# Batch 2 of a fused attention and MLP kernel: q loaded in plain form, cast by GpSimd and turned by TensorE

## The chip, the cores and the metric

The kernel runs on one core of one Trainium2 chip. The metric is the device time of one execution in microseconds (us), lower is better. The core has five engines that work side by side, each with its own queue of instructions that it takes strictly in order: TensorE (PE: matmuls and transposes by matmul; its weight loads are shown apart as PEld), VectorE (DVE), ScalarE (ACT), GpSimd (POOL) and SyncE (SP). They wait for one another by semaphores. Transfers (DMAs) are issued from an engine's queue; here SP issues plain and transposing transfers, and POOL issues those that cast float32 to bfloat16 on the way.

## The reference

Decayed causal attention, and then a SiLU MLP on its output:

```python
# q, k, v: 8 batches x 8 heads x 576 tokens x 64; f: 8 x 8 x 576
scores = (1 / sqrt(64)) * q @ k.T
cum = cumsum(log(clip(f, 1e-4, 1)))            # along the tokens
scores = where(causal, -1e9, scores + cum[:, None] - cum[None, :])
attn = softmax(scores)
x = (attn @ v), heads side by side             # 4608 tokens x 512
h = x @ w_in                                   # 512 x 2048
out = (h * sigmoid(h)) @ w_out                 # 2048 x 512 -> 4608 x 512, float32
```

## The kernel before

**Tiling.** Two heads of one batch make a pair, whose 2 x 64 columns fill 128 partitions. There are 32 pairs, p = 0 to 31; batch b holds pairs 4b to 4b+3. The 576 tokens of a head are five blocks of 128, 128, 128, 128 and 64. The scores are made transposed (keys on partitions, queries along the free axis), so q and k are needed with the head dimension on partitions: tiles qT (two buffers, one per batch) and kT (two constant tiles, by turns). `scores(p, t)` (L267) makes one of four groups t of score blocks by matmul (L278), which ScalarE turns into exponentials (L303). `attend_rows` (L334) multiplies them with v, which GpSimd has scaled by the decay and given a column of ones (`prep_v`, L243). The result is divided by its row sum on VectorE (L355, L356) and turned into columns of xT, by TensorE (`turn_pair`, L363, with ScalarE copies L374) in the first batches. xT is cut into nine groups g of 512 tokens for the MLP: `m1_chunk` (L388) makes one of 16 chunks of a group's hidden layer (four matmuls L397, tanh on ScalarE L408, product on VectorE L409), `m2_part` (L416) a quarter of one output tile of 128 tokens (four matmuls L422, then ScalarE L431 and a store by SP, L435).

**How q and k come to be turned.** Batches 0 and 1 (`NEARLY = 2`) take the first way: `load_main` and `load_tail` load them from SP as float32, tokens on partitions, rows of 1 KB, into a tile `whole` (q and k side by side, from the two buffers tagged gtile that later hold the hidden layer too) and a tile `raw` for the last 64 tokens. `cast_both` (L556) has GpSimd cast a pair's q and k to bfloat16 (L190 the main part, L199 the tail). `transposes(p, which)` (L224) has TensorE turn five blocks (L232) into a PSUM tile tpqk of the four buffers tagged big, and VectorE copies that into qT or kT (L237, L241). Batches 2 to 7 take the second way: `load_qk` (L120) loads one block of all eight heads from POOL's queue with a cast to bfloat16 into a tile mp, and `turn_qk` (L128) has SP issue a transposing transfer from mp into qT or kT (L132).

**The order of the work** is written out by hand, in `manual_schedule`: the order in the program is the order on each engine. After pairs 0 to 3 a loop over p = 4 to 31 (L639) takes each pair through: transfers planned for this p (the table `plan`: turns, loads of v), `scores(p, 0)` and `(p, 1)`, some MLP work, for p up to 6 `transposes(p + 1, 0)`, `attend_rows(p - 1)`, `prep_v(p + 1)`, for p up to 5 `cast_both(p + 2)`, the POOL loads planned for this p (the table `fetch`), `scores(p, 2)` and `(p, 3)`, and more MLP work. `pace` says how many MLP pieces a pair gets. `can_m1` lets the first half of a group's MLP run at most two groups ahead of the second half. For batch 2, the fetches stand at p = 4 (blocks 0 and 1) and p = 5 (blocks 2, 3, 4), the turns at p = 6 and p = 7, and the first use at p = 8.

Of the kernel before, what the change touches and what calls it, by code (L numbers as in the profile page):

```python
# [19 lines left out]
def kernel(  # L20
# [12 lines left out]
    B, H, S, D = q.shape  # L33
# [9 lines left out]
    NPB = H // 2  # L43
# [28 lines left out]
    tpool = ctx.enter_context(tc.tile_pool(name="tpool", bufs=3))  # L72
    opool = ctx.enter_context(tc.tile_pool(name="opool", bufs=4))
    NEARLY = 2
    NTURN = 4
    LAG = 10.0
    MOST = 9.0
# [8 lines left out]
    def raw_tile():  # L86
        return stp.tile([P, DM], FP32, name="raw", tag="raw")
# [4 lines left out]
    def load_main(b, h0, h1):  # L92
        if b not in whole:
            whole[b] = gpool.tile(
                [P, 2, H, (NB - 1) * D], FP32, name="whole", tag="gtile"
            )
        for which, src in enumerate((q, k)):
            nc.sync.dma_start(  # L98
                out=whole[b][:, which, h0:h1, :],
                in_=src[b, h0:h1, 0:SM, :].rearrange("h (p c) d -> p h (c d)", c=NB - 1),  # L100
            )

    def load_tail(b):
        for which, src in enumerate((q, k)):
            t = raw_tile()
            tails[b, which] = t.rearrange("s (h d) -> s h d", h=H)
            nc.sync.dma_start(
                out=tails[b, which][:TAIL, :, :],
                in_=src[b, :, SM:S, :].rearrange("h s d -> s h d"),
            )  # L110
# [86 lines left out]
    def cast_tail(b, j, which):  # L197
        m = cast[b, j, which]
        nc.gpsimd.tensor_copy(  # L199
            out=m[:TAIL, NB - 1, :, :], in_=tails[b, which][:TAIL, 2 * j : 2 * j + 2, :]  # L200
        )
# [236 lines left out]
    m2_queue = [(g, tb, pt) for g in range(NG) for tb in range(4) for pt in range(4)]  # L438
    m1_ready = 0
# [16 lines left out]
    def can_m1():  # L456
        if not m1_queue:
            return False
        g = m1_queue[0][0]
        return g < m1_ready and (not m2_queue or m2_queue[0][0] > g - 2)  # L460

    def can_m2():
        return bool(m2_queue) and (not m1_queue or m1_queue[0][0] > m2_queue[0][0])
# [14 lines left out]
    def have():  # L478
        return sum(1 for x in m1_queue + m2_queue if x[0] < m1_ready)

    def pace(p):
        b, j = divmod(p, NPB)
        if b < NEARLY:
            return have() / (NPB - j)
# [32 lines left out]
    def add(to, at, fn, *args):  # L517
        to.setdefault(at, []).append(lambda: fn(*args))

    for b in range(NEARLY, B):  # L520
        for i, group in enumerate([(0, 1), (2,), (3, 4)]):
            at = NPB * b - 4 + min(i, 1) if b == NEARLY else NPB * b - 7 + i
            for c in group:
                for w in range(2):
                    add(fetch, at, load_qk, b, c, w)
                    if b <= NEARLY + 1:
                        add(plan, at + (2 if b == NEARLY else 3), turn_qk, b, c, w)
                    elif i == 0 and b - 2 >= NTURN:
                        add(plan, NPB * b - 4, defer, 9.0, partial(turn_qk, b, c, w))
                    else:  # L530
                        add(plan, NPB * b - 4 + min(i, 1), turn_qk, b, c, w)
                add(plan, NPB * b - 5 + i + (b == NEARLY), load_v, b, c, nc.sync)

# [11 lines left out]
    with tc.manual_schedule():  # L545
        nc.scalar.dma_start(out=f_sb[:, :], in_=f.rearrange("b h s -> (b h) s"))
        load_main(0, 0, 2)
        load_tail(0)
        load_main(0, 2, 4)
        for c in range(2):  # L550
            load_v(0, c, nc.sync)
        load_main(0, 4, H)
        for c in range(2, NB):
            load_v(0, c, nc.sync)

        def cast_both(p):  # L556
            b, j = divmod(p, NPB)
            for w in range(2):
                cast_main(b, j, w)
            for w in range(2):  # L560
                cast_tail(b, j, w)

        make_identity(nc, ident_bf)
        make_upper_triangular(nc, mask01, val=1.0, diag=True)
        make_identity(nc, ident_f)
        for kT in kTs:
            nc.vector.memset(kT[:, :, S:], 0.0)
        for u in us:
            nc.vector.memset(u[:, :, uoff[4] + TAIL :], 0.0)
        for va in vaugs:  # L570
            nc.vector.memset(va[:, NB - 1, :, :], 0.0)
        nc.vector.memset(wT[:, NB - 1, :], 0.0)
        nc.vector.tensor_scalar(
            out=maskadd[:, :], in0=mask01[:, :], scalar1=1.0, scalar2=1e30,
            op0=ALU.subtract, op1=ALU.mult,
        )
        decay_clip()
        LO, HI = ((0, 3),), ((3, NB),)
        for w in range(2):
            cast_main(0, 0, w)  # L580
        for w in range(2):
            cast_tail(0, 0, w)
        cast_both(1)
        cast_both(2)
        load_w(w_in_bf, moe_w_in, 0, DFF // 2)
        load_w(w_in_bf, moe_w_in, DFF // 2, DFF)
        for w in range(2):
            turn_first(w)
        scores(0, 0)
        turn_first_tails()  # L590
        scores(0, 1)
        decay_sum()
        scores(0, 3)
        transposes(1, 0)
        scores(0, 2)
        decay_turn()
        prep_v(0)
        transposes(1, 1)
        scores(1, 0)
        cast_both(3)  # L600
        load_tail(1)
        load_main(1, 0, 4)
        load_main(1, 4, H)
        for c in range(NB):
            load_v(1, c, nc.sync)
        for p in range(1, NPB):
            more = p + 1 < NPB
            prep_v(p)
            scores(p, 1)
            if more:  # L610
                transposes(p + 1, 0)
            scores(p, 3)
            if more:
                transposes(p + 1, 1)
            if p > 1:
                turn_pair(p - 2)
            attend_rows(p - 1, LO)
            scores(p, 2)
            if more:
                scores(p + 1, 0)  # L620
            attend_rows(p - 1, HI)
        turn_pair(NPB - 2)
        attend_rows(NPB - 1, LO)
        attend_rows(NPB - 1, HI)
        m1_chunk(0, 0, begin=True)
        turn_pair(NPB - 1)
        m1_ready = 1
        cast_both(NPB)
        cast_both(NPB + 1)
        prep_v(NPB)  # L630
        for c in range(0, NFC, NFC // 4):
            load_rows(w_out_bf, moe_w_out, c, c + NFC // 4)
        work(HOLD)
        transposes(NPB, 0)
        work(1)
        transposes(NPB, 1)
        work(2)
        due = 0.0
        for p in range(NPB, NP):  # L639
            b, j = divmod(p, NPB)  # L640
            early = b < NEARLY
            for fn in plan.get(p, []):
                fn()
            due += pace(p)
            n = int(due)
            due -= n
            n1, n2 = (n + 2) // 3, (n + 1) // 3
            n3 = n - n1 - n2
            scores(p, 0)
            scores(p, 1)  # L650
            spend(0.4)
            work(n1)
            ahead = p + 1 < NPB * NEARLY
            rows = NPB < p < NPB * NEARLY
            if ahead:
                transposes(p + 1, 0)
            if rows:
                attend_rows(p - 1, LO)
                spend(0.6)
            if p + 1 < NP:  # L660
                prep_v(p + 1)
            if p + 2 < NPB * NEARLY:
                cast_both(p + 2)
            for fn in fetch.get(p, []):
                fn()
            if early:
                work(n2 // 2)
            scores(p, 2)
            scores(p, 3)
            spend(0.3)  # L670
            if ahead:
                transposes(p + 1, 1)
            if rows:
                attend_rows(p - 1, HI)
            work(n2 - n2 // 2 if early else n2)
            if b >= NEARLY and j > 0:
                attend_rows(p - 1)
                spend(1.2)
            work(n3)
            if j > 0 and b < NTURN:  # L680
                turn_pair(p - 1)
            if j == NPB - 1:
                attend_rows(p)
                spend(1.2)
                if b < NTURN:
                    work(2)
                    turn_pair(p)
                    ready(p)
                else:
                    retire(p)  # L690
        while m1_queue or m2_queue or later:
            n = len(m1_queue) + len(m2_queue)
            work(1)
            if n == len(m1_queue) + len(m2_queue):
                spend(1.0)
# [28 lines left out]
```

## Time and profile before

| | |
|---|---|
| median of 3 runs | 363.94 us (363.58 to 365.53) |
| the profiled execution | 366.61 us, of which the profile's span is 364.8 us |
| mean granted TensorE clock in it | 0.984 |
| PE busy | 339.6 us (93% of the span) |
| ACT, DVE, POOL busy | 212.1, 189.7, 120.5 us |

The profiled execution is 2.7 us longer than the median of the runs, and 1.8 us of it lie outside the span. In the views below a line of the timeline holds the start, the duration, the engine, the line of the kernel, the operation and its tiles, the count, and in brackets how long the engine had been idle before and what ended that. A DMA issue on a queue (SPq, POOLq, POOL) shows the issuing, not the transfer. The line PEclk is the clock that was granted to TensorE in each of 40 equal slices of the span, in tenths of full speed.

### The profile page before, as it was taken

Reading aid. Unit: us, or ns where it says so; the run is one execution under the profiler, and the core shown is the slowest. Engines: PE = TensorE matmul, PEld = TensorE weight load, DVE = VectorE, ACT = ScalarE, POOL = GpSimd, SP = SyncE. Lnnn points to the kernel's source line nnn. Section 1 sums busy time; section 2 is a strip of 40 time slices with the busy share of each in tenths; the row PEclk is TensorE's granted clock in tenths of the full one; section 3 lists DMA queues with packets and bytes.
Section 4 is the critical chain, followed back from the end, with each engine's and each line's share of the span. In section 5 each row is a group of like instructions: output and inputs, shape, how many; then the busy total and the mean of one; then the engine's idle time right before and its main releaser. Section 6 shows DMA issues by size and latency. Waiting matters only on the chain.

```text
span 364.8 us, 7023 instructions
## 1 busy us (share of the span) xinstructions
PE 339.6 (93%) x2677; PEld 167.1 (46%) x2677; DVE 189.7 (52%) x442; ACT 212.1 (58%) x345; POOL 120.5 (33%) x204
## 2 busy tenths in 40 slices
PE   2798979947999999999999999999999999999995
PEld 1355435522455545554454444444544454444442
DVE  4764894422763387236832784358436832843410
ACT  4566764624974687567746784667367723744421
POOL 5563499466035704561454362011301000000000
PEclk9999999985999999999999999999999999999999
DMA  8899899999969799879979998453050014000012
GB/s 220 200 207 313 186 187 178 132 159 208 192 63 159 110 178 120 102 53 193 158 79 184 125 120 184 106 105 102 30 124 29 2 58 118 8 31 29 29 64 82
DMA packets 148082, 44.92 MB, mean 123 GB/s; under 512 B 136208, under 2 KB 142352, under 8 KB 148048
## 3 DMA queue, kind: packets, MB, share of 16 engines
q1 hardware_dynamic: 88544, 33.05, 42.3%
q0 software_dynamic: 59424, 11.28, 41.1%
q8 instruction: 21, 0.34, 0.4%
q10 hardware_dynamic: 80, 0.15, 0.1%
q14 instruction: 13, 0.11, 0.1%
HBM read 36.85 MB, written 9.44 MB: 127 GB/s over the span
## 4 chain that ended last, share of the span: by engine, by line
PE 75%; DMA 10%; SPq 7%; ACT 2%; POOL 2%; issue 1%; DVE 1%; ACTq 0%; DVEq 0%
PE hp L397 31%; PE po L422 31%; PE sc L278 6%; PE avr L346 6%; DMA w_out_bf<-in_moe_w_out_dram 3%; SPq L115 3%; DMA mp<-in_k_dram 3%; SPq L98 3%; SPq L132 2%; DMA qT<-mp 2%; ACT uT L303 1%; DMA vm<-in_v_dram 1%; DMA whole<-in_k_dram 1%; PE tpx L368 1%; POOL vaug L248 1%
## 5 line engine op out<-in xcount | busy, mean ns | idle before, releaser
L397 PE MATMUL hp<-xT,w_in_bf 128*128 128x512 bf16 x576 | 139.5, 385 | 1.1 <-ACT xT L374 0.7
L422 PE MATMUL po<-w_out_bf,gtile 128*128 128x512 bf16 x576 | 136.6, 379 | 0.9 <-DVE gtile L409 0.6
L409 DVE SCALAR_TENSOR_TENSOR gtile<-th,hp 128x512 bf16<-128x512 bf16 x144 | 96.3, 685 | 55.3 <-ACT th L408 53.1
L303 ACT ACTIVATE uT<-sc 128x1024 bf16<-128x1024 f32 (+1 forms) x128 | 101.2, 849 | 30.3 <-PE sc L278 21.6
L408 ACT ACTIVATE th<-hp 128x512 bf16<-128x512 f32 x144 | 85.0, 612 | 51.0 <-PE hp L397 48.2
L248 POOL TENSOR_TENSOR vaug<-vm,wT 128x512 bf16<-128x512 f32 x64 | 45.5, 733 | 140.7 <-PE avr L346 120.3
L397 PEld LDWEIGHTS <-w_in_bf 128*128 128x128 bf16 x576 | 53.5, 99 | 65.7 <-issue 8.6
L422 PEld LDWEIGHTS <-gtile 128*128 128x128 bf16 x576 | 53.6, 98 | 63.6 <-issue 3.2
L317 DVE TENSOR_TENSOR uT<-uT,mask 128x256 bf16<-128x256 bf16 (+1 forms) x112 | 35.8, 341 | 72.8 <-ACT uT L303 72.6
L431 ACT ACTIVATE osb<-po 128x512 f32<-128x512 f32 x36 | 21.7, 602 | 47.3 <-PE po L422 47.3
L278 PE MATMUL sc<-qT,kT 64*128 64x64 bf16 (+4 forms) x384 | 37.6, 288 | 12.2 <-DMA qT<-mp 6.5
L346 PEld LDWEIGHTS <-uT 128*128 128x128 bf16 x960 | 33.7, 98 | 7.1 <-issue 1.3
L346 PE MATMUL avr<-vaug,uT 128*128 128x65 bf16 x960 | 36.2, 195 | 0.7 <-POOL vaug L256 0.7
L278 PEld LDWEIGHTS <-kT 64*128 64x128 bf16 x384 | 15.1, 95 | 38.8 <-issue 24.0
L356 DVE TENSOR_TENSOR xt<-avr,rr 128x384 bf16<-128x384 f32 x64 | 31.4, 491 | 2.3
L123 POOL DMA_DIRECT2D mp<-in_q_dram x30 | 26.6, 887 | 0.0
L123 POOL DMA_DIRECT2D mp<-in_k_dram x30 | 25.9, 862 | 0.3 <-PE sc L278 0.3
L355 DVE RECIPROCAL rr<-avr 128x6 f32<-128x6 f32 x64 | 11.6, 182 | 19.0 <-PE avr L346 18.8
L374 ACT COPY xT<-tpx 128x512 bf16<-128x512 bf16 (+7 forms) x32 | 11.2, 404 | 17.2 <-PE tpx L368 17.2
L190 POOL CAST m<-whole 128x512 bf16<-128x512 f32 x16 | 9.8, 628 | 15.2 <-DMA whole<-in_q_dram 12.1
L368 PE MATMUL tpx<-ident_bf,xt 128*128 128x128 bf16 (+1 forms) x80 | 9.0, 216 | 1.3 <-DVE xt L356 1.1
L368 PEld LDWEIGHTS <-xt 128*128 128x128 bf16 (+1 forms) x80 | 6.2, 96 | 6.5 <-DVE xt L356 2.3
(47 smaller groups left out, 65.4 us busy)
## 6 DMA issues: line engine op xcount, KB each, us to landing
out_dram<-osb SPq DMA_DIRECT2D x36, 256.0 KB, 2.2
vm<-in_v_dram SPq DMA_DIRECT2D x32, 256.0 KB, 5.0
mp<-in_q_dram POOLq DMA_DIRECT2D x24, 128.0 KB, 5.5
mp<-in_k_dram POOLq DMA_DIRECT2D x24, 128.0 KB, 6.2
w_in_bf<-in_moe_w_in_dram POOLq DMA_DIRECT2D x2, 1024.0 KB, 11.2
w_out_bf<-in_moe_w_out_dram POOLq DMA_DIRECT2D x4, 512.0 KB, 9.7
whole<-in_q_dram SPq DMA_DIRECT2D x3, 512.0 KB, 10.9
whole<-in_k_dram SPq DMA_DIRECT2D x3, 512.0 KB, 9.6
```

The costliest lines, as they stand in the source:

```text
L123: nc.gpsimd.dma_start(out=t[: bs[c], :].rearrange("p (h d) -> p h d", h=H), in_=(q, k)[which][b, :, c * P : c * P + bs[c], :].rearrange("h ...
L248: nc.gpsimd.tensor_tensor(out=va[:n, c0:c1, :, 0:D], in0=vm[:n, c0:c1, 2 * j : 2 * j + 2, :], in1=wT[:n, c0:c1, 2 * j + b * H : 2 * j + 2 ...
L278: nc.tensor.matmul(sc[:, i, col : col + n], lhsT=kT[r, kb * P : (kb + 1) * P], rhs=qT[r, q0 : q0 + n], start=True, stop=not pe_adds,)
L303: nc.scalar.activation(out=u[:, :, o : o + col], in_=sc[:, :, 0:col], func=ACT.Exp, scale=scale)
L317: nc.vector.tensor_tensor(out=d, in0=d, in1=mk, op=ALU.mult)
L346: nc.tensor.matmul(av[:, qb - lo, i, :], lhsT=u[:, i, o : o + P], rhs=va[:, kb, i, :], start=(kb == 0), stop=(kb == qb),)
L356: nc.vector.tensor_tensor(out=xt[:, lo:hi, 2 * j : 2 * j + 2, :], in0=av[:, :, :, 0:D], in1=r[:, 0:n, :, None].to_broadcast([P, n, 2, D]), ...
L397: nc.tensor.matmul(hp[:, :], lhsT=w_in_bf[:, cc, fc * P : (fc + 1) * P], rhs=xg[g][:, cc, :], start=(cc == 0), stop=(cc == NCC - 1),)
L408: nc.scalar.activation(out=th[:, :], in_=hp[:, :], func=ACT.Tanh, scale=0.5)
L409: nc.vector.scalar_tensor_tensor(out=gte[:, fc, :], in0=th[:, :], scalar=1.0, in1=hp[:, :], op0=ALU.add, op1=ALU.mult,)
L422: nc.tensor.matmul(po[:, :], lhsT=gte[:, fc, tb * P : (tb + 1) * P], rhs=w_out_bf[:, fc, :], start=(fc == 0), stop=(fc == NFC - 1),)
L431: nc.scalar.activation(out=osb[:, :], in_=po[:, :], func=ACT.Copy, scale=0.5)
```

## The change

A table `RAW` says which of q (0) and k (1) of a batch take the first way. Batches 0 and 1 have both, as before, and batch 2 has q. So five casting loads and five transposing transfers of q fall away, and in their place come three plain loads from SP after pair 5's casts (the tail, heads 0 to 3, heads 4 to 7), one cast of main part and tail per pair on GpSimd at p = 6 to 9, and five transposes with two VectorE copies per pair at p = 7 to 10. The five loads and the five turns of k stay, with the turns now all at p = 6 (blocks 2 to 4 stood at p = 7). Batch 2's `whole` takes one more turn of the two gtile buffers, and a new term in `can_m1` keeps the first half of group 1 from starting before the second half of group 0 is through.

```diff
     NEARLY = 2
+    RAW = {0: (0, 1), 1: (0, 1), 2: (0,)}
...
-        for which, src in enumerate((q, k)):
+        for which in RAW[b]:
+            src = (q, k)[which]
             nc.sync.dma_start(
                 out=whole[b][:, which, h0:h1, :],
...
     def load_tail(b):
-        for which, src in enumerate((q, k)):
+        for which in RAW[b]:
+            src = (q, k)[which]
             t = raw_tile()
...
-        return g < m1_ready and (not m2_queue or m2_queue[0][0] > g - 2)
+        return g < m1_ready and (not m2_queue or m2_queue[0][0] > max(g - 2, min(g - 1, 0)))
...
             at = NPB * b - 4 + min(i, 1) if b == NEARLY else NPB * b - 7 + i
+            late = 1 if b == NEARLY + 1 and len(RAW[NEARLY]) == 2 else 0
             for c in group:
                 for w in range(2):
-                    add(fetch, at, load_qk, b, c, w)
+                    if w in RAW.get(b, ()):
+                        continue
+                    add(fetch, at + late, load_qk, b, c, w)
                     if b <= NEARLY + 1:
-                        add(plan, at + (2 if b == NEARLY else 3), turn_qk, b, c, w)
+                        to = min(at + late + (2 if b == NEARLY else 3), NPB * b - 2)
+                        add(plan, to, turn_qk, b, c, w)
...
-            for w in range(2):
+            for w in RAW[b]:
                 cast_main(b, j, w)
-            for w in range(2):
+            for w in RAW[b]:
                 cast_tail(b, j, w)
...
-            ahead = p + 1 < NPB * NEARLY
+            ahead = RAW.get((p + 1) // NPB, ())
             rows = NPB < p < NPB * NEARLY
-            if ahead:
+            if 0 in ahead:
                 transposes(p + 1, 0)
...
-            if p + 2 < NPB * NEARLY:
+            if (p + 2) // NPB in RAW:
                 cast_both(p + 2)
+            if p == NPB * NEARLY - 3:
+                load_tail(NEARLY)
+                load_main(NEARLY, 0, 4)
+                load_main(NEARLY, 4, H)
             for fn in fetch.get(p, []):
                 fn()
...
-            if ahead:
+            if 1 in ahead:
                 transposes(p + 1, 1)
```

On TensorE the order of everything else stays as it was: twenty transposes are put in, five each at p = 7, 8, 9 and 10, and nothing is moved. ScalarE's order is the same throughout.

## The prediction

> **What bounds the kernel now.** I read the page's busy line and the 40 slices first, then TensorE's waits, then the timeline of TensorE and of SP around the one place where TensorE is not full.
>
> ```profile
> PE   2798979947999999999999999999999999999995
> PEclk9999999985999999999999999999999999999999
> ```
>
> Each slice is 9.1 us. From the third slice on TensorE is nearly full, but for slice 9 (73 to 82 us), at 4 tenths. The clock dips in slices 9 and 10. After them TensorE is full to the end: the stretch 91 to 300 us has 207.99 us of TensorE busy in 209.00. So whatever is won or lost before 91 us goes to the end unless a new wait takes it up.
>
> TensorE's waits (total, times, longest), after 77 us alone:
>
> ```profile
> PE sc L278 <- DMA qT<-mp: 6.5, 2, 5.1
> PE sc L278 <- ACT uT L303: 0.5, 1, 0.5
> PE hp L397 <- DVE gtile L409: 0.3, 1, 0.3
> PE tpx L368 <- DVE xt L356: 0.2, 1, 0.2
> ```
>
> The timeline of TensorE about that wait:
>
> ```profile
> 77.25 0.36 PE L368 MATMUL tpx<-ident_bf,xt 128*128 128x128 bf16 x2 [0.21 <-DVE xt L356]
> 82.70 0.61 PE L278 MATMUL sc<-qT,kT 64*128 64x512 bf16 x2 [5.09 <-DMA qT<-mp]
> 84.70 0.61 PE L278 MATMUL sc<-qT,kT 64*128 64x64 bf16 x4 [1.39 <-DMA qT<-mp]
> 85.25 5.15 PE L397 MATMUL hp<-xT,w_in_bf 128*128 128x512 bf16 x12
> 90.33 0.42 PE L278 MATMUL sc<-qT,kT 64*128 64x320 bf16 x6
> ...
> 95.10 0.61 PE L278 MATMUL sc<-qT,kT 64*128 64x512 bf16 x6
> 95.64 2.76 PE L397 MATMUL hp<-xT,w_in_bf 128*128 128x512 bf16 x12
> 98.34 0.42 PE L278 MATMUL sc<-qT,kT 64*128 64x320 bf16 x6
> ```
>
> Pair 8, the first of batch 2, stands 5.09 us for its turned q, then 1.39 us more, and its twelve hp matmuls take 5.15 us where pair 9's take 2.76: a granted clock of 0.52 from 85.2 to 90.3 us, 1.00 after it.
>
> Why q is late stands in SP's queue:
>
> ```profile
> 70.83 0.94 SPq L435 DMA_DIRECT2D out_dram<-osb  x1
> 71.87 2.14 SPq L132 DMA_TRANSPOSE qT<-mp  x1
> 74.11 1.44 SPq L132 DMA_TRANSPOSE kT<-mp  x1
> 75.64 1.22 SPq L132 DMA_TRANSPOSE qT<-mp  x1
> 76.95 1.61 SPq L132 DMA_TRANSPOSE kT<-mp  x1
> 78.65 1.20 SPq L132 DMA_TRANSPOSE qT<-mp  x1
> 79.96 2.13 SPq L132 DMA_TRANSPOSE kT<-mp  x1
> ```
>
> The turns of blocks 2 to 4 stand behind a store that waits for MLP output until 70.83, are issued one after the other, and land 6.0 to 8.4 us later. `scores(8, 0)` needs q of blocks 0 to 3 but k of block 0 only, `scores(8, 1)` q of block 4.
>
> **The change part by part.** Pairs are named by p; times are those of the profiled execution before.
>
> *The stall.* From the end of tpx (77.61) to `scores(8, 2)` (90.33) is 12.72 us. The same work in pair 9, 95.10 to 98.34, is 3.24 us. With q turned by TensorE at p = 7 and k's turns all at p = 6, before the store of 70.83, I take away 12.72 - 3.24 = 9.5 us. Counted the other way, waits of 5.09 + 1.39 and 5.15 - 2.76 of clock, it is 8.9; these are the ends.
>
> *k's turns.* k blocks 0 and 1 stay at p = 6; POOL issues k 2 to 4 at about 54.0 to 56.6. The software queue is in order in this trace: w_out's last quarter lands at 57.83, the first q load (issued 49.15) 9.5 us later at 58.65, the next three about 0.9 us apart. So k 0 to 4 land by about 63, SP issues their turns from 60.1 (behind the store of 59.56) to about 67, and with the longest landing of such a turn (9.2) they are there at 76: before 77.6. Cost 0.
>
> *Twenty transposes on TensorE.* In batch 1 a group starts at 44.06 and the next hp at 44.51, or at 61.36 with avr at 61.81: 0.45 us. The alike tpx group takes 0.32 start to start (103.18 to 103.50); 0.53 is its listed duration. Ends 1.3 and 2.1, taken 4 x 0.45 = 1.8 us, all on the path. In 42 to 54 us, with three such groups, the clock is 1.00. The Trainium skill, page TensorE: Matmul & The Clock Gate, section Part 4: PE-mode transpose, speaks against this: about 275 ns for one transpose in a kernel, and transposes do not count as activity for the clock. By it the twenty cost 5.5 us (an estimate) and the sum would come out at 361.4. No row here shows a transpose that slow or a clock that dips for one, so I stay with the rows.
>
> *VectorE's copies* are 4 x (0.68 + 0.17) = 3.4 us. In pair 9 (95.1 to 103.5) VectorE is busy 6.98 of 8.40 us; with 0.85 it has 7.8 of 8.85, so TensorE's MLP work hides them. *ScalarE* gets nothing new, but pair 8 no longer has slack: exponentials 3.2, eight tanh 4.8 and the copies of pair 7 0.7 make 8.7 us, against 3.24 + 0.45 + 4.77 (90.33 to 95.10) = 8.5 on TensorE. Four PSUM buffers carry hp, and pair 9 has less for ScalarE (6.74 of 8.40 busy). Ends 0 and 1.5 (the two waits of tanh for VectorE amid the first transposes, 37 to 42 us, where TensorE lost nothing), taken 0.4.
>
> *The plain loads of q.* Two q issues fewer at p = 4 (0.95 + 0.90) put pair 7's casts, 54.20 to 55.84 before, at 52.4 to 54.0. SP, idle from 41.5 to 59.5, then issues tail, heads 0 to 3 and heads 4 to 7 from 54.0 to 56. Batch 1's like loads landed 10.3, 10.9 and 12.9 us after issue, with w_in on its way beside them. So heads 0 to 3 are there at 54.6 + 10.9 = 65.5. Beside them w_out's last 3.8 us run, for which TensorE already waits 0.36 us at 57.88. Ends 0 and 3.8 (shared half and half from the first issue). While w_out ran alone the engines moved 161 to 184 GB/s, in 20 to 30 us with both queues at work 221, so they have room: taken 0.8, nearer zero.
>
> *GpSimd.* It issues five loads fewer (4.5 us) and casts 4 x (0.63 + 0.26) = 3.6 us. Pair 8's cast waits for the plain load until 65.5 and ends at 66.4; behind it stand two loads for batch 3 (66.25 before as well) and `prep_v(8)`. TensorE comes to `transposes(8, 0)` at 70.0: 3.6 us to spare, and still 1.5 with the longest landing in the trace (13.0). Pair 9's cast stands behind `prep_v(8)`, which starts at 76.32 and waits in its second part until 77.57 for v of batch 2; that load keeps about its place on SP (four turns ahead of block 3; one turn between blocks 3 and 4, where there was none). So this cast ends at about 79, TensorE needs it at 77.6 + 3.24 = 80.85, or 0.8 later with w_out. Ends 0 and 4, taken 0.3. Casts 10 and 11 have over 4 us.
>
> *Later.* Batch 3's last turn is issued at 101.91 and pair 12 starts at 123.22, over 20 us on; 6 us less is still covered. Its turns also come up earlier, since SP is rid of batch 2's. The new term of `can_m1` changes no place in TensorE's order; its hidden-layer buffers wait only for work long past.
>
> *Sum*: -9.5 + 1.8 + 0.4 + 0.8 + 0.3 = -6.2 us. The profiled 366.61 becomes 360.4; it stands 2.67 above the median of the runs, so from 363.94 I forecast 357.7 us. The ends of the terms give -8.2 to +2.5 if all bad ends came together, which I don't expect.
>
> **The rivals.** *A second wait takes part of the gain*: v of batch 2, pair 9's cast or w_out comes 2 to 4 us late, since the plain q loads now share the engines in 54 to 67 us (share of the DMA engines 2.26 in 60 to 68). For it: only 1.5 us at pair 9, and 0.36 already waited for w_out. Against it: five casting loads and five turns less. It gives 359.5 to 362.
>
> *Slower than before*: heads 0 to 3 of q land so late that TensorE stands at `transposes(8, 0)`, and the cast holds up GpSimd's queue. Each us after 69.1 costs one, and a wait near 5 us brings the half clock, 2.4 us more, as it did at 82.7. The 6.2 are gone at a wait of 3.8 + 2.4; 0.5% slower needs about 5.6, a landing at 74.7, 20 us after issue. The longest in the trace is 13.0. Price 366 or more.
>
> *It does not do what it says*: `scores(8, 0)` then waits for kT instead, if k's turns at p = 6 are held up (k 2 to 4 must have landed before SP goes on to v). A landing of 13.0 for k block 3 would put its turn at 68, and kT block 3 is only needed at `scores(8, 2)`. Price: 3 to 6 us of the stall stays, 361 to 364.
>
> **How the numbers follow.** The main case, no new wait over 2 us, has 0.72, with its own range 355.7 to 359.5 (gains of 8.2 and 4.4). The partial wait has 0.15, the kT wait 0.07, the slower case 0.05, and 0.01 is left below. A change of 0.5% is 1.8 us, about what a measurement here tells from no change: faster than 362.1 is 0.72 + 0.15 + some of the kT case = 0.88, same 0.07, slower 0.05. The range reaches from the main case's best to the end of most partial waits: 355.0 to 361.5.
>
> **What would show it.** Right: no TensorE wait for qT, the clock line without the 8 and 5, pair 8 taking about 8.5 us from its first score to pair 9's, four tpqk groups at 0.3 to 0.5 us, GpSimd's cast of pair 8 ending before 70. Wrong: a TensorE wait named by tpqk and m (the cast), by w_out, or by kT; ScalarE or VectorE named ahead of hp in 78 to 95 us; a new dip of the clock. The weakest step is how long plain loads take beside the rest in 54 to 67 us.

## The result, and the profile after

The changed kernel takes 360.22 us (median of 4 executions, 359.25 to 361.6) against 364.74 us for the kernel before (4 executions, 363.58 to 366.72). The ratio is 0.9861, with a 95% interval of 0.9827 to 0.9895; the quotient of these two medians is 0.9876. So the kernel is 1.2 to 1.4% faster, 4.5 to 5.1 us. The forecast was 357.7 us: the gain came, and was 1 to 2 us smaller than the 6.2 us forecast. Ratios, here and below, leave out an execution that took over 1.5% longer than the fastest of the same kernel, while medians and ranges count all.

The profiled execution after takes 359.25 us, with a span of 357.5 us against 364.8 before. First the slices of its page, as read before (PE busy, granted clock):

```profile
PE   2797989999999999999999999999999999999995
PEclk9999999999999999999999999999999999999999
```

The slice at 4 tenths is gone, and so is the dip of the clock. TensorE's waits, the longest of the whole execution:

```profile
PE tpqk L211 <- POOL m L193: 5.3, 2, 4.5
PE sc L281 <- ACT uT L306: 2.2, 5, 0.5
PE sc L281 <- DVE kT L240: 1.8, 2, 1.0
PE tpx L371 <- DVE xt L359: 1.1, 3, 0.6
PE sc L281 <- DVE kT L212: 0.8, 1, 0.8
PE hp L400 <- DVE gtile L412: 0.8, 2, 0.4
```

There is no wait for qT by a transfer any more. What is left comes from the start (the first line, 4 us into the execution) and from short waits, most of which the kernel before has too (the wait of hp for gtile has grown, from 0.3 us to 0.8). The timeline of TensorE at pair 8 and pair 9 (start, duration, engine, line, operation, count; in brackets the idle time before):

```profile
77.41 0.36 PE L371 MATMUL tpx<-ident_bf,xt 128*128 128x128 bf16 x2 [0.21 <-DVE xt L359]
77.58 0.63 PE L281 MATMUL sc<-qT,kT 64*128 64x512 bf16 x6
78.14 2.76 PE L400 MATMUL hp<-xT,w_in_bf 128*128 128x512 bf16 x11
80.74 0.52 PE L235 MATMUL tpqk<-ident_bf,m 128*128 128x128 bf16 x5
81.07 0.44 PE L281 MATMUL sc<-qT,kT 64*128 64x320 bf16 x6
81.62 3.61 PE L400 MATMUL hp<-xT,w_in_bf 128*128 128x512 bf16 x16
85.68 1.02 PE L400 MATMUL hp<-xT,w_in_bf 128*128 128x512 bf16 x4 [0.44 <-DVE gtile L412]
86.64 0.61 PE L281 MATMUL sc<-qT,kT 64*128 64x512 bf16 x6
```

Pair 8 starts as soon as pair 7's last transposes are through, its hp matmuls take 2.76 us in place of 5.15, and pair 9 starts at 86.64 in place of 95.10. Of these 8.46 us, 7.82 are left when pair 11 starts (103.99 against 111.81), after two more groups of transposes, and 7.3 at the end. Between pair 8's first score and pair 9's lie 9.06 us, 0.44 of them a wait of hp for VectorE. The chain of work that ended last shows what VectorE did before it: products for the MLP (gtile) until 82.76, the copies of pair 9's turned q until 83.46, two products with the causal mask until 85.03, and then the gtile that hp waited for. So the new copies stand in the way of hp here. ScalarE's tanh just ahead of that gtile ended at 85.01, so the trace does not tell which of the two engines set the time.

The other side of it, GpSimd's casts of pairs 8 and 9 with what stands ahead of them:

```profile
61.39 0.61 POOL L193 CAST m<-whole 128x512 bf16<-128x512 f32 x1 [0.15 <-DMA whole<-in_q_dram]
61.94 0.29 POOL L202 CAST m<-raw 64x128 bf16<-64x128 f32 x1
...
76.64 1.04 POOL L251 TENSOR_TENSOR vaug<-vm,wT 128x512 bf16<-128x512 f32 x1 [11.61 <-PE avr L349]
78.18 0.40 POOL L251 TENSOR_TENSOR vaug<-vm,wT 64x128 bf16<-64x128 f32 x1 [0.50 <-DMA vm<-in_v_dram]
78.52 0.22 POOL L259 CAST vaug<-wT 128x10 bf16<-128x10 f32 x1
78.66 0.60 POOL L193 CAST m<-whole 128x512 bf16<-128x512 f32 x1
```

Pair 8's cast begins at 61.39, over 8 us before TensorE turns it (69.71). Pair 9's cast stands behind the wait for v and ends 1.2 us before its transposes at 80.74.

### The profile page after: what moved, and what is told of

Read it like the earlier page. It is cut to its first block, busy times and chain, and to the rows that moved or that the text cites. A ratio compares the mean times of both kernels' runs of the same rounds, so it can differ in the third digit from the quotient of the medians.

```text
span 357.5 us, 7026 instructions
## 1 busy us (share of the span) xinstructions
PE 336.3 (94%) x2656; PEld 168.4 (47%) x2697; DVE 191.7 (54%) x450; ACT 211.9 (59%) x345; POOL 119.6 (33%) x207
## 4 chain that ended last, share of the span: by engine, by line
PE 82%; DVE 6%; ACT 4%; DMA 3%; issue 3%; POOL 1%; SPq 0%; ACTq 0%
PE po L425 33%; PE hp L400 30%; PE avr L349 7%; PE sc L281 7%; DVE gtile L412 2%; ACT uT L306 2%; DMA xT<-xt 2%; PE tpx L371 2%; DVE uT L320 2%; PE tpqk L235 2%; ACT th L411 1%; DMA whole<-in_k_dram 1%; DVE xt L359 1%; PE sc L289 1%; DVE qT L240 1%
## 5 line engine op out<-in xcount | busy, mean ns | idle before, releaser
L400 PE MATMUL hp<-xT,w_in_bf 128*128 128x512 bf16 x556 | 135.8, 380 | 3.2 <-DVE gtile L412 0.8
L425 PE MATMUL po<-w_out_bf,gtile 128*128 128x512 bf16 x555 | 133.7, 379 | 1.4 <-DVE gtile L412 0.4
L126 POOL DMA_DIRECT2D mp<-in_q_dram x25 | 22.2, 887 | 1.3 <-DMA w_out_bf<-in_moe_w_out_dram 0.5
L193 POOL CAST m<-whole 128x512 bf16<-128x512 f32 x20 | 11.9, 607 | 15.0 <-DMA whole<-in_q_dram 12.4
L235 PE MATMUL tpqk<-ident_bf,m 128*128 128x128 bf16 (+1 forms) x90 | 10.9, 241 | 0.3 <-DVE gtile L412 0.3
L235 PEld LDWEIGHTS <-m 128*128 128x128 bf16 (+1 forms) x90 | 7.3, 106 | 6.3 <-issue 1.6
```

The costliest lines, as they stand in the source:

```text
L126: nc.gpsimd.dma_start(out=t[: bs[c], :].rearrange("p (h d) -> p h d", h=H), in_=(q, k)[which][b, :, c * P : c * P + bs[c], :].rearrange("h ...
L235: nc.tensor.transpose(tp[:, c * P : c * P + n], m[:n, c, :, :].rearrange("p h d -> p (h d)"), ident_bf[:n, :n],)
L400: nc.tensor.matmul(hp[:, :], lhsT=w_in_bf[:, cc, fc * P : (fc + 1) * P], rhs=xg[g][:, cc, :], start=(cc == 0), stop=(cc == NCC - 1),)
L425: nc.tensor.matmul(po[:, :], lhsT=gte[:, fc, tb * P : (tb + 1) * P], rhs=w_out_bf[:, fc, :], start=(fc == 0), stop=(fc == NFC - 1),)
```

## The experiments

The theory: the kernel before stands still because q's turns come late, for their place in SP's queue; q out of the queue, or early in it, ends that. The change then pays for twenty transposes and their copies. The rivals: the transfers themselves are too slow, whatever their place; VectorE or ScalarE become the bound; the gain of the profiled execution is not that of most.

**The changed kernel once more**, with no edit.

> The changed kernel once more, to size the gain with more runs. The traces of before and after differ by 7.3 us in span, the medians by 4.5 us. If the stall is the same in most executions of before, this shows a gain of 5 to 7.5 us (0.980 to 0.986). Rival: the stall of before varies from run to run, and the gain with it; then the runs of before spread by 3 us or more and the gain is 3 to 5 us.

Measured: 360.08 us (6 executions, 357.35 to 362.43) against 365.18 (17 executions, 362.08 to 367.03); ratio 0.9862 (0.981 to 0.9914). The gain is 5.1 us, just over the lower bound of the theory's 5 to 7.5, while the ratio lies 0.0002 above its 0.986. The kernel before does spread by 5 us, as the rival says, so this run lies on the border of the two. The spread goes along with the clock: of the 62 executions of the kernel before beside the runs of this study, 44 had a mean granted clock of 0.990 or more and a median of 364.6 us, 16 had 0.986 or less and a median of 366.2. Whether a longer stall brings the lower clock or the other way round, these figures don't tell. The profiled execution before had 0.984; of the 62, one was lower and two were the same.

**Only the turns moved**, q still by casting loads and transposing transfers:

```diff
-                        add(plan, at + (2 if b == NEARLY else 3), turn_qk, b, c, w)
+                        add(plan, min(at + (2 if b == NEARLY else 3), NPB * b - 2), turn_qk, b, c, w)
```

> The kernel before with one thing moved: the turns of blocks 2 to 4 of batch 2 stand at p = 6, ahead of the store that SP waits for until 70.8, instead of p = 7. q still goes through casting loads and transposing transfers. Theory (the place in SP's queue makes most of the stall): ten turns in a row from 60.1 us at 1.3 us each; q's block 3 is issued at about 68 and lands at 75 to 77, q's block 4 at 78 to 80. The first wait of pair 8 (5.1 us) falls to 0 to 1, the second stays at 1 to 2, no half clock: 5 to 8 us faster than before. Rival (the number of casting and transposing transfers is what is slow): the turns still land at 80 or later, and 0 to 3 us are won.

Measured: 361.25 us, but from 356.88 to 364.15 in 6 executions; ratio 0.9856 (0.9792 to 0.9919) without the two longest, 362.39 and 364.15. The profiled one is the longest; TensorE in it:

```profile
77.48 0.39 PE L278 MATMUL sc<-qT,kT 64*128 64x512 bf16 x2
80.78 0.40 PE L278 MATMUL sc<-qT,kT 64*128 64x64 bf16 x4 [2.90 <-DMA qT<-mp]
81.11 4.45 PE L397 MATMUL hp<-xT,w_in_bf 128*128 128x512 bf16 x11
```

The first scores no longer wait, as forecast; q's last block, ninth of ten turns and issued at 74.68, still holds the second ones for 2.9 us, and a clock of 0.66 from 81 to 86 us follows. So moving the turns alone wins 3.9 us at the median of all six and 5.3 by the ratio, about as much as the change (0.9861), but it spreads more: the best execution is faster than any of the changed kernel, the worst nearly as slow as the kernel before. That the second wait makes the difference is likely, but not shown: the shorter executions left no trace.

**k's turns of blocks 2 to 4 put back** behind the store, in the changed kernel:

```diff
-                        to = min(at + late + (2 if b == NEARLY else 3), NPB * b - 2)
+                        to = at + late + (2 if b == NEARLY else 3)
```

> The changed kernel with k's turns of blocks 2 to 4 put back to p = 7, behind the store. q stays with TensorE. Theory (q's way is what matters, since the first scores need q of all blocks but k of blocks 0 and 1 only): these turns are issued from 73.3 us, land at 80 to 82, and only the third group of scores of pair 8 (at 81) waits, 0 to 2 us: 0 to 2 us slower than the changed kernel. Rival (the place in SP's queue is what matters): most of the stall comes back, 5 us or more slower than the changed kernel.

Measured: 359.35 us (358.7 to 359.71), ratio 0.9843 (0.9797 to 0.9889): no slower than the changed kernel. TensorE never waits for a turn of k. For k's blocks 2 to 4 the place behind the store did no harm; it was q, of which the first scores need every block, that had to be early.

**k loaded plainly too** (by the change's line with `late`, batch 3's casting loads then also come one pair later):

```diff
-    RAW = {0: (0, 1), 1: (0, 1), 2: (0,)}
+    RAW = {0: (0, 1), 1: (0, 1), 2: (0, 1)}
```

> The changed kernel with k of batch 2 also loaded in plain form and turned by TensorE. Theory (with the stall gone every further group of transposes only costs): four more groups at 0.33 to 0.45 us on TensorE, four more copies of 0.85 us on VectorE and so a longer wait in pair 8: 1.5 to 3 us slower than the changed kernel. Rival (the DMA engines still hold something back in 54 to 78 us, such as v of batch 2): 0 to 2 us faster than it.

Measured: 362.8 us (12 executions, 361.22 to 366.81), 2.7 us slower than the changed kernel, ratio 0.9952 to before (0.9916 to 0.9988). The profile names a price besides the transposes: a TensorE wait of 1.7 us at pair 7's start for VectorE's copy of kT, and behind it a clock of 0.61 from 69.9 to 74.0 us. Turning k on TensorE too would have taken back about half of what turning q gives.

**Each group of q turned twice**, to measure the price:

```diff
             if 0 in ahead:
                 transposes(p + 1, 0)
+                if p + 1 >= NPB * NEARLY:
+                    transposes(p + 1, 0)
```

> The changed kernel with each of batch 2's four q groups turned and copied twice (the second time into the same place). It measures the price of the change itself. Theory: five transposes cost 0.33 to 0.45 us on TensorE, and VectorE's 0.85 us per group adds a wait in pair 8 alone: 1.3 to 2.5 us slower than the changed kernel (360.1). Rival (VectorE and ScalarE bound pairs 8 to 10): 4 us or more slower, with TensorE waits named by gtile or qT in 78 to 105 us.

Measured: 361.94 us (361.49 to 362.69), 1.9 us more than the changed kernel's 360.1, ratio 0.9929 (0.991 to 0.9948), against 0.9862 a difference of 2.4 us. TensorE in its pair 8:

```profile
81.25 0.52 PE L235 MATMUL tpqk<-ident_bf,m 128*128 128x128 bf16 x5
82.43 0.52 PE L235 MATMUL tpqk<-ident_bf,m 128*128 128x128 bf16 x5 [0.67 <-DVE gtile L412]
```

Elsewhere two groups stand back to back, 0.8 to 1.0 us for ten transposes. Pair 11 starts 2.17 us later in this profile than in that of the changed kernel (106.16 against 103.99). So four more groups cost about 2 us with everything that hangs on them; that the first four cost the same is an estimate. A wait for VectorE of 0.67 us appears in pair 8 and one of 0.24 in pair 9, none in pairs 10 and 11. The 4 us of the rival, VectorE and ScalarE as the bound, did not come.

**The plain loads late**, at p = 6 behind k's turns:

```diff
             for fn in plan.get(p, []):
                 fn()
+            if p == NPB * NEARLY - 2:
+                load_tail(NEARLY)
+                load_main(NEARLY, 0, 4)
+                load_main(NEARLY, 4, H)
...
-            if p == NPB * NEARLY - 3:
-                load_tail(NEARLY)
-                load_main(NEARLY, 0, 4)
-                load_main(NEARLY, 4, H)
```

> The changed kernel with its three plain loads of q issued at p = 6, behind k's turns and the loads of v, in place of p = 5. It tests what the rival of a slower kernel would have cost. Theory: SP issues them at about 72 us, heads 0 to 3 land at 80 to 84, and TensorE stands from 70 to 81 or 85 before it turns q of pair 8, with half clock after it: 13 to 17 us slower than the changed kernel, 8 to 12 us slower than before. Rival (there is slack elsewhere, or the loads land faster in a quieter stretch): 5 to 10 us slower than the changed kernel.

Measured: 366.65 us (10 executions, 364.78 to 368.36), ratio 1.0056 (1.0029 to 1.0083): 6.6 us slower than the changed kernel, in the rival's 5 to 10. SP, GpSimd and TensorE:

```profile
69.49 1.16 SPq L100 DMA_DIRECT2D whole<-in_q_dram  x2
```

```profile
74.17 0.61 POOL L193 CAST m<-whole 128x512 bf16<-128x512 f32 x1 [13.56 <-DMA whole<-in_q_dram]
```

```profile
74.84 0.60 PE L235 MATMUL tpqk<-ident_bf,m 128*128 128x128 bf16 x5 [4.50 <-POOL m L193]
```

The loads were issued at 69, not 72, and heads 0 to 3 landed after 4.6 us, not 10, in a stretch where GpSimd had stopped issuing loads of its own. TensorE stood 4.5 us, and the mean clock from 66 to 78 us was 0.88. This execution also waits 1.31 us for kT at 221 us, as the profile of the changed kernel does not; whether the edit brings that is open. The case in which the change loses is real: a landing at 74.2 makes it 0.56% slower than before.

**The stall filled**, in the kernel before, with matmuls that nobody reads:

```diff
+            if p == NPB * NEARLY:
+                fill = big([P, TG], FP32, "fill")
+                for _ in range(24):
+                    nc.tensor.matmul(
+                        fill[:, :], lhsT=w_in_bf[:, 0, 0:P], rhs=w_in_bf[:, 0, 0:TG],
+                        start=True, stop=True,
+                    )
             scores(p, 0)
             scores(p, 1)
```

> The kernel before, with 24 matmuls of 512 columns that nobody reads (5.2 us) put ahead of pair 8's first scores, where TensorE stood 5.1 us. It splits the stall into wait and clock. Theory (the half clock comes from the standing still, and is part of the price): the waits shrink to 0 to 1.5 us, the twelve hp matmuls of pair 8 take 2.8 us, the mean clock rises from 0.991 to 0.997 or more, and it is 1 to 2.5 us faster than before. Rival (the wait alone is the price): 0 to 2 us slower than before, since in executions with a shorter stall the filling is too long.

Measured: 363.37 us (12 executions) against 364.57 (23), ratio 0.9965 (0.9946 to 0.9983).

```profile
77.33 5.35 PE L652 MATMUL fill<-w_in_bf 128*128 128x512 bf16 x23
82.62 0.39 PE L278 MATMUL sc<-qT,kT 64*128 64x512 bf16 x2
84.28 0.40 PE L278 MATMUL sc<-qT,kT 64*128 64x64 bf16 x4 [1.27 <-DMA qT<-mp]
84.61 2.76 PE L397 MATMUL hp<-xT,w_in_bf 128*128 128x512 bf16 x12
```

With 5.35 us of useless work the kernel gets 1.2 us faster, since the twelve hp matmuls behind it run at full clock, 2.76 us. The clock is a part of the stall's price of its own, at least 1.2 us.

**q's turns first, and batch 3's loads later**, with the kernel before as the base: no transposes of batch 2 on TensorE at all.

```diff
+    for c, w in ((0, 0), (0, 1), (1, 0), (1, 1)):
+        add(fetch, NPB * NEARLY - 4, load_qk, NEARLY, c, w)
+    for c, w in ((2, 0), (3, 0), (4, 0), (2, 1), (3, 1), (4, 1)):
+        add(fetch, NPB * NEARLY - 3, load_qk, NEARLY, c, w)
+    for c, w in ((0, 0), (0, 1), (1, 0), (2, 0), (3, 0), (4, 0), (1, 1), (2, 1)):
+        add(plan, NPB * NEARLY - 2, turn_qk, NEARLY, c, w)
...
-            at = NPB * b - 4 + min(i, 1) if b == NEARLY else NPB * b - 7 + i
+            at = NPB * b - 7 + i + (b == NEARLY + 1)
...
+                    if b == NEARLY:
+                        continue
                     add(fetch, at, load_qk, b, c, w)
                     if b <= NEARLY + 1:
-                        add(plan, at + (2 if b == NEARLY else 3), turn_qk, b, c, w)
+                        add(plan, min(at + 3, NPB * b - 2), turn_qk, b, c, w)
...
+                if b == NEARLY and c > 2:
+                    add(plan, NPB * NEARLY - 2, turn_qk, NEARLY, c, 1)
```

> The kernel before, with q kept on casting loads and transposing transfers, but all of batch 2's turns at p = 6 and q's ahead of k's of blocks 1 to 4, q's casting loads ahead of k's, and batch 3's casting loads one pair later. Theory (q only had to be early): q's last block is issued at about 68 us and lands by 77, no wait for qT, and no transposes on TensorE: 1 to 2 us faster than the changed kernel (358 to 359). Rival (the DMA engines are too full in 58 to 78 us for ten turns): pair 8 still waits 2 us or more for qT or now for kT, and it is no faster than the changed kernel.

Measured: 356.77 us (356.55 to 358.61), ratio 0.9799 (0.9775 to 0.9823), 3.3 us faster than the changed kernel (2.3 by the two ratios), more than expected. SP and TensorE:

```profile
62.84 6.66 SPq L132 DMA_TRANSPOSE qT<-mp  x4
69.59 2.52 SPq L132 DMA_TRANSPOSE kT<-mp  x2
```

```profile
77.03 0.61 PE L278 MATMUL sc<-qT,kT 64*128 64x512 bf16 x6
77.57 2.76 PE L397 MATMUL hp<-xT,w_in_bf 128*128 128x512 bf16 x11
80.27 0.42 PE L278 MATMUL sc<-qT,kT 64*128 64x320 bf16 x6
```

All of q's turns are issued by 69.5, and pair 8 waits for nothing.

**The same with batch 3's loads where they were:**

```diff
-            at = NPB * b - 7 + i + (b == NEARLY + 1)
+            at = NPB * b - 7 + i
```

> The kernel of e7, with batch 3's casting loads back at their old pairs (5, 6, 7 in place of 6, 7, 8). It asks whether e7 owes its time to the order of the turns alone. Theory (the order on SP's queue is what counts, q's turns ahead of the store and of k's): no wait for qT or under 1 us, 356.5 to 358.5. Rival (the four casting loads of batch 3 that then share the engines hold the turns up): a wait of 2 us or more for qT or kT in pair 8, 359 to 362.

Measured: 359.44 us (358.45 to 361.06), ratio 0.9837 (0.981 to 0.9864). Pair 8 has no wait for qT and one for kT, whose last block was issued at 78.0:

```profile
82.38 0.20 PE L278 MATMUL sc<-qT,kT 64*128 64x64 bf16 x2 [0.85 <-DMA kT<-mp]
```

The time lies in the rival's range, the waits are the theory's. So the order of loads and turns alone wins what the change wins (0.9837 against 0.9861).

**Batch 3's loads later alone**, in the kernel before (their turns then come at p = 9 and 10 in place of 8 to 10):

```diff
-            at = NPB * b - 4 + min(i, 1) if b == NEARLY else NPB * b - 7 + i
+            at = NPB * b - 4 + min(i, 1) if b == NEARLY else NPB * b - 7 + i + (b == NEARLY + 1)
...
-                        add(plan, at + (2 if b == NEARLY else 3), turn_qk, b, c, w)
+                        add(plan, at + 2 if b == NEARLY else min(at + 3, NPB * b - 2), turn_qk, b, c, w)
```

> The kernel before, with batch 3's casting loads one pair later and nothing else: the turns of batch 2 stay where they were, blocks 2 to 4 behind the store of 70.8 us. Theory (the order on SP's queue): the turns still start at about 71 and only land sooner, in 4 to 6 us in place of 6 to 8.4; 1 to 3 us of the stall go, half clock or not, 361.5 to 363.5. Rival (full DMA engines are the cause of the late turns): most of the stall goes, 357 to 360.

Measured: 363.16 us (362.36 to 364.82) against 366.05, ratio 0.9927 (0.9904 to 0.995). In SP's queue the first of the late turns goes out at 70.99 (71.87 before) and each takes 1.2 us to issue in place of 1.2 to 2.1. Pair 8's first scores no longer wait, but its second ones do:

```profile
82.30 0.61 PE L278 MATMUL sc<-qT,kT 64*128 64x64 bf16 x4 [4.47 <-DMA qT<-mp]
```

The clock still dips (0.64 from 82.3 to 87.0). Batch 3's loads beside the turns lengthen the stall by 2 to 3 us, but don't make it.

**Batch 3's loads later in the changed kernel**, and the best kernel once more beside it:

```diff
-            late = 1 if b == NEARLY + 1 and len(RAW[NEARLY]) == 2 else 0
+            late = 1 if b == NEARLY + 1 else 0
```

> The changed kernel with batch 3's casting loads one pair later. It asks why e7 is 3.3 us faster than the changed kernel, where the price of turning q on TensorE was 1.9 us by e4. Theory (with q loaded plainly nothing that TensorE waits for is late any more, so emptier DMA engines give nothing): within 0.7 us of the changed kernel, 359.5 to 360.5, and the remaining difference to e7 is TensorE's transposes and scatter. Rival (the casting loads of batch 3 hold up something in the changed kernel too): 1.5 us or more faster than the changed kernel, 357 to 358.5.

> The kernel of e7 once more, beside e10 on the same chip. Theory (q early by transposing transfers, without TensorE's transposes): 356 to 358, 1.5 to 3.5 us faster than e10. Rival (e7's first time was a favourable draw of the pair 8 wait, as the 356.9 to 364.2 of e1 were): 358 to 361 with a wide spread.

Measured: 359.8 us (358.91 to 364.44, ratio 0.987, 0.9829 to 0.9911) and 357.51 us (356.55 to 358.48, ratio 0.9801, 0.977 to 0.9832). Batch 3's loads out of the way give the changed kernel 0.3 us, nothing that can be told from scatter. The difference of 2.3 us to the best kernel stands beside the 2 us or so of transposes.

## Why the prediction was right, point by point

- **The forecast**: 360.22 us is inside the stated range, but beyond the main case's own 355.7 to 359.5 and in that of the partial wait (359.5 to 362), and the profile shows no second wait of 2 to 4 us. 0.8 us of the 2.5 come from the kernel before, which took 364.74 in place of 363.94; the rest is the gain.
- **The stall and its cause**: right. It is gone after, and the runs show the cause from both sides: q early by transposing transfers (359.44) does what q by TensorE does (360.08), and k left behind the store costs nothing (359.35).
- **The size of the stall, 9.5 us**: this term was mis-sized. It is right for the profiled execution (8.46 us won at pair 9 with one group of transposes at p = 8 and the 0.44 us wait already paid, so 9.2). But that execution had one of the lowest clocks of the kernel before. With a gain of 5.1 us at the medians and a price of about 2, the stall cost about 7 us in a typical one, an estimate; the best kernel, which has neither the stall nor the transposes, is 7.3 us faster than the kernel before by its ratios. The prediction saw that the profiled execution stood 2.67 us above the median, and carried the whole term over all the same.
- **The transposes, 1.8 us, and ScalarE's 0.4**: 1.9 to 2.4 measured for both together by doubling them. In the timeline a group among hp matmuls takes 0.33 us start to start (80.74 to 81.07), nearer the tpx row than the 0.45 taken; the one ahead of avr takes 0.45 (69.71 to 70.16).
- **VectorE's copies hidden**: not in pair 8. Its 0.44 us wait is of the size of the 0.4 taken for ScalarE, but the chain ahead of it goes through VectorE's new copies. That is also one of the prediction's own signs of being wrong, VectorE named ahead of hp, if a small one.
- **The page on transposes**: of the Trainium skill, page TensorE: Matmul & The Clock Gate, section Part 4: PE-mode transpose, the 275 ns for one transpose was no price here, where five took 0.33 to 0.46 us start to start. Its remark that transposes do not count for the clock was not tested: the clock was 1.00 through the doubled groups, but these are 1.2 us at most amid matmuls.
- **w_out, 0.8 us**: 0 in the profiled execution, where TensorE does not wait for it at all; 0.8 in that of the run with k's turns put back. Within its ends, of the size taken in one execution and nothing in another.
- **Pair 8's cast**: earlier than worked out, 61.39 in place of 65.5, since heads 0 to 3 were issued at 53.0, not 54.6, and landed in 8.2 us, not 10.9. **Pair 9's**: it ended 1.2 us ahead of TensorE, where the prediction had 1.5 to spare (1.85 by its own working, 80.85 less 79), and cost nothing in place of 0.3.
- **k's turns, cost 0**: right; no wait for a turn of k in the profile after. The working was early: the last turn left SP's queue at 71.4, not 67, and landed at 77.3, 3.8 us before block 4 of k is needed (81.07).
- **The slower rival**: its turning point held. The prediction had 0.5% slower than before at a landing of 74.7; the experiment with late loads landed at 74.2 and was 0.56% slower (0.29 to 0.83). What I expected of that run itself was wrong by half, because I took landing times from a crowded stretch for one that the edit itself had emptied.

## What to carry to other kernels

A transfer that the first work of a stage needs whole goes ahead of those it needs in parts, and ahead of any store that waits for compute on the same queue: the order alone was worth as much here as a new path for the data. A stall of some microseconds costs its length and the slow clock behind it, and both differ from one execution to the next, so size a term that holds a stall on more than one execution. If a cheaper order gives the same, the extra engine work of the new path (here about 2 us) is a loss.

## What the runs showed of the hardware that I had not expected

A much shorter wait than 5 us can bring the half clock, in some executions. In the profile of the changed kernel's second run, pair 5 waits 1.96 us for a copy by VectorE (1.0 in the first), and the next eight hp matmuls take 3.41 us in place of 1.90:

```profile
51.12 0.74 PE L281 MATMUL sc<-qT,kT 64*128 64x512 bf16 x6 [1.96 <-DVE kT L240]
51.79 3.41 PE L400 MATMUL hp<-xT,w_in_bf 128*128 128x512 bf16 x8
```

The granted clock was 0.57 from 51.1 to 55.1 us, and pair 8 starts 2.1 us later than in the first run. The length of the wait alone does not decide it: in the profile with k loaded plainly too, pair 5 waits 1.81 us and the next eight hp matmuls take 1.90, while pair 7 waits 1.74 us and the next eight po matmuls take 3.34. The small wait of pair 5 is in every profile here (0.34 to 1.96 us), so it can be one source of the scatter; how often it brings the slow clock was not measured, and what decides it stays open.
